# Residual of six blocks: one accumulating DMA for each block, in place of GpSimd's adds

## The chip, the core and the metric

The kernel runs on one core of one Trainium2 chip. The core has five engines that work side by side and wait for one another by semaphores: TensorE (PE in the profile) multiplies matrices into PSUM, VectorE (DVE) and ScalarE (ACT) empty PSUM and do elementwise work, GpSimd (POOL) does elementwise work and issues DMAs, and SyncE (SP) issues DMAs. DMAs move data between HBM (where inputs and outputs lie) and SBUF, and within SBUF. The metric is the device time of one execution in microseconds, the median over runs. A profile is of one execution; its span runs from the first to the last instruction.

## The reference

Attention with 16 beacon keys in front of 576 causal keys, for 8 batches and 8 heads of width 64, then a mixer on the attention's result x (8 x 576 rows of 512):

```
scores = scale * q @ k_all.T                 # k_all: beacons, then tokens; causal mask on tokens
a      = exp(scores - max) / (sum + 1e-9)
x      = a @ v_all                            # heads side by side: (batch, 576, 512)
h      = x.T @ U @ V                          # rank 32, along the 576 tokens
u      = x + h.T
out    = u + relu(u @ w_ch1) @ w_ch2          # 512 -> 2048 -> 512, float32
```

The last line matters here: `out` is the sum of the residual u and the second layer's product. The kernel takes float32 and computes with float16 operands and float32 sums.

## The kernel before, in words

**Two streams of work.** Attention runs batch by batch and head pair by head pair. The mixer runs on the 4608 rows of all batches, in 9 blocks of 512 rows (t = 0 to 8); a block can begin when u of its rows is there. The units of the mixer's blocks (a few matmuls and what goes with them) stand in a list `queue`; `fill(n)` (L1269) takes n units from it, and the attention code calls `fill` between its own steps. So TensorE gets attention and mixer work in turn, in an order fixed when the program is built. Every engine runs its own instructions in that order.

**Two more lists go with the units.** `storing` (L1108) holds stores with a countdown: after every unit `fill` lowers the countdown of all entries, and calls those at the front that have fallen below zero. `coming` holds loads of later batches (k, q, v and beacons, all issued by GpSimd, which converts them from float32 to float16) and some sums of weights; `fill` calls one of them after every unit.

**Where u comes from.** For each batch from the third on, SyncE transposes x into the ring `uT` (L456, five DMA transposes), TensorE multiplies the low-rank part into four PSUM banks (`most`, L490) and one for the last rows (`end`, L503), and VectorE adds those onto `uT` (L477). The blocks' first layer reads `uT` as its moving operand (L675, L701).

**A block (`fast_units`, L622).** The first layer gives 2048 x 512 values `gT`, with ReLU. The second layer uses seven half-size products in place of eight (sums of operands on VectorE ahead, sums of products behind). Blocks 1 to 6 do this by `c_unit` and `after`; in blocks 7 and 8, called `quads`, another order (`chain_units`) ends the run. A block's result comes in four quarters of 256 rows x 256 columns: "11", "22", "21" and "12", in this order; a quarter is one tile `ob` (128 x 2 x 256 float32; pool `outp`, four buffers). VectorE, or ScalarE in some blocks for "11" (L926), writes the product into `ob`.

**The residual.** `out` wants u in row order. So SyncE transposes the block's part of `uT` into a float16 tile `ut` (128 x 4 x 512; pool `utp`, two buffers; L640), four DMA transposes that go out with the units of the block's first layer. `residual` (L860) then has GpSimd add the right quarter of `ut` to `ob` in four pieces of 128 columns (`in_pieces`, L571; the instruction's line is L577), and `store` (L851) puts the store of the quarter into `storing` with a countdown of 2; SyncE issues it (L854). Blocks 7 and 8 call `residual` for "11" alone; their other quarters get u by VectorE (`begun`). Block 0 has its own code (L1010) without `residual`.

**GpSimd's order.** Its queue holds, in the order in which the program was built: the loads of `coming`, the adds of `residual`, the sums of weights (L615). An add that waits for `ob` holds the loads behind it.

Of the kernel before, what the change touches and what calls it, by code (L numbers as in the profile page):

```python
# [14 lines left out]
ALU = mybir.AluOpType  # L15
# [3 lines left out]
P = 128  # L19
# [11 lines left out]
def kernel(  # L31
# [13 lines left out]
    nc = tc.nc  # L45
# [525 lines left out]
    def in_pieces(o, x, y, op, n=4):  # L571

        h = o.shape[1]
        w = o.shape[2] * h // n
        for i in range(h):
            for c in range(0, o.shape[2], w):
                nc.gpsimd.tensor_tensor(  # L577
                    out=o[:, i, ds(c, w)], in0=x[:, i, ds(c, w)], in1=y[:, i, ds(c, w)], op=op
                )
# [42 lines left out]
    def fast_units(t0, dst, last=False, parts=0, ahead=None):  # L622


        cell, banks, obs = {}, {}, {}
        few = PARTS.get(t0 // 512 + 1, 0) == 1
        quads = t0 // 512 >= NBLK - 2
# [209 lines left out]
        def u_of(h, c):  # L837
            return cell["u"][:, ds(2 * h, 2), ds(HC * c, HC)]
# [12 lines left out]
        def store(name, h, c, i=None, c0=0, w=HC):  # L851
            if i is None:
                both = dst(2 * h, 2 * P)[:, ds(HC * c, HC)].rearrange("(k p) c -> p k c", p=P)
                u = lambda t=obs[name]: nc.sync.dma_start(out=both, in_=t)  # L854
                storing.append([2, u]) if not last else u()
            else:
                eng = nc.scalar if name == "21" or i and not c0 else nc.sync
                eng.dma_start(out=dst(2 * h + i, P)[:, ds(HC * c + c0, w)], in_=obs[name][:, i, ds(c0, w)])

        def residual(name, h, c):  # L860
            in_pieces(obs[name], obs[name], u_of(h, c), ALU.add)
            store(name, h, c)

        def after(k):
            if k == 0:
                nc.scalar.activation(out=kept("s1"), in_=banks["A"], func=AF.Copy)
                freed("A")
            elif k == 1:
                add(out_tile("11"), banks["F"], cell["s1"])
                freed("F")  # L870
                residual("11", 0, 0)
            elif k == 2:
                add(kept("u2"), banks["B"], cell["s1"])
                freed("B")
            elif k == 3:
                add(kept("u3"), banks["C"], cell["u2"])
                freed("C")
            elif k == 4:
                add(out_tile("22"), banks["D"], cell["u3"])
                residual("22", 1, 1)  # L880
            elif k == 5:
                add(out_tile("21"), banks["E"], cell["u3"])
                freed("E")
                residual("21", 1, 0)
            else:
                add(out_tile("12"), banks["D"], cell["u2"])
                freed("D")
                residual("12", 0, 1)
# [219 lines left out]
    coming, storing = [], []  # L1108
# [186 lines left out]
    def feed(b):  # L1295

        while state["t"] < NBLK and 512 * (state["t"] + 1) <= S * (b + 1):
            t = state["t"]
            dst = lambda i, m, t=t: rows[ds(512 * t + P * i, m), :]
            if t < FAST:  # L1300
                units, state["part"] = mlp_units(512 * t, 512, dst, t % 2, t > 0)
                if t == FAST - 1:
                    for i, u in zip(DIFFS, halves_of_w2()):
                        units[i] = lambda a=units[i], u=u: (a(), u())
            else:
                units = fast_units(512 * t, dst, t == NBLK - 1, PARTS.get(t, 0), sums_ahead(t + 1))
            queue.extend(units)
            state["t"] += 1
# [40 lines left out]
    with tc.manual_schedule(engines={ENG.PE, ENG.Activation, ENG.DVE, ENG.SP, ENG.Pool}):  # L1349
# [191 lines left out]
        for p in range(NP1, NP):  # L1541
            b, c = divmod(p, NH2)
# [127 lines left out]
```

## Time and profile before

| | |
|---|---|
| Median of 3 runs | 332.73 us (332.49 to 332.76) |
| The profiled execution | 332.49 us, span 330.7 us |
| Granted TensorE clock, mean | 0.996 |
| Instructions in the span | 9280 |
| HBM read, written | 37.45 MB, 9.44 MB |
| Share of the chain that ended last | PE 91%, ACT 4%, DVE 1%, DMA 1% |

How to read the rows that follow. A row by group names line, engine, operation, output <- inputs (names of tiles, buffer numbers left out), shapes, count, then busy time in us, mean ns of one instruction, and the engine's idle time just before them with what ended it. A row of the timeline or of the chain begins with its start and its length in us. A row of waits reads: who, at which line, waited for what: total us, times, longest. A DMA row gives the issuing queue, the count, the size and the median us from issue to landing. In a table by stretches each engine's busy time is followed by its number of instructions. Queue q0 carries GpSimd's DMAs, q1 those of SyncE.

### The profile page before, as it was taken

How to read it: one execution, taken by the hardware profiler on the slowest of the kernel's cores; microseconds unless marked ns; L12 is line 12 of the kernel's file. 1: busy time of each engine (PE TensorE's matmuls, PEld its weight loads, DVE VectorE, ACT ScalarE, POOL GpSimd, SP SyncE). 2: the span in 40 equal slices, each digit the busy share in tenths (PEclk: the TensorE clock that was granted, in tenths of full speed). 3: DMA queues.
4: the chain of work that ended last, by engine and by line, in shares of the span. 5: the costliest groups of instructions: out<-in, count | busy, mean ns of one | idle time of the engine just before them, and what ended most of it. 6: DMA issues, size and time to landing. Idle time of an engine off the chain costs nothing.

```text
span 330.7 us, 9280 instructions
## 1 busy us (share of the span) xinstructions
PE 322.6 (98%) x3660; PEld 228.1 (69%) x3660; DVE 264.7 (80%) x608; ACT 196.4 (59%) x430; POOL 166.7 (50%) x263
## 2 busy tenths in 40 slices
PE   7899999999999999999999999999999999999994
PEld 3564555555578656876588888765787888788783
DVE  6776988679998668786878777877788898798993
ACT  5957962789972677348844695379636613703700
POOL 8987724766238960689058923950283036030030
PEclk9999999999999999999999999999999999999998
DMA  7999999999999996999999999995014313405003
GB/s 164 142 179 143 185 201 194 200 187 155 80 129 166 215 130 106 111 162 138 148 149 162 146 135 160 92 211 81 10 65 120 70 44 101 63 11 166 18 10 125
DMA packets 150561, 41.99 MB, mean 127 GB/s; under 512 B 131312, under 2 KB 149936, under 8 KB 150512
## 3 DMA queue, kind: packets, MB, share of 16 engines
q0 software_dynamic: 87568, 18.18, 73.1%
q1 hardware_dynamic: 62144, 22.41, 37.4%
q10 hardware_dynamic: 800, 0.75, 0.7%
q8 instruction: 30, 0.49, 0.7%
q14 instruction: 19, 0.16, 0.2%
HBM read 37.45 MB, written 9.44 MB: 142 GB/s over the span
## 4 chain that ended last, share of the span: by engine, by line
PE 91%; ACT 4%; DVE 1%; DMA 1%; issue 0%; ACTq 0%
PE gps L675 21%; PE mpsA L909 9%; PE po L428 8%; PE qpsA L701 6%; PE mpsD L829 6%; PE sps L410 6%; PE cps L1053 4%; PE gps L1027 4%; PE mpsE L829 3%; PE mpsC L829 3%; PE mpsB L829 3%; PE qpsD L701 3%; ACT expt L377 2%; PE mpsF L829 2%; PE mpsD L909 2%; ACT w L377 2%
## 5 line engine op out<-in xcount | busy, mean ns | idle before, releaser
L577 POOL TENSOR_TENSOR ob<-ob,ut 128x128 f32<-128x128 f32 x104 | 50.0, 511 | 121.9 <-DVE ob L849 59.4
L419 ACT ACTIVATE expt<-sps 128x496 f16<-128x496 f32 (+2 forms) x192 | 82.0, 539 | 41.8 <-PE sps L410 41.8
L675 PE MATMUL gps<-uT,w 128*128 128x512 f16 (+1 forms) x368 | 78.1, 351 | 0.0
L829 PEld LDWEIGHTS <-gT 128*128 128x128 f16 x576 | 54.2, 98 | 8.8 <-issue 2.6
L675 PEld LDWEIGHTS <-w 128*128 128x128 f16 x368 | 33.2, 98 | 25.6 <-issue 1.3
L653 DVE TENSOR_TENSOR gT<-gT 128x1024 f16<-128x1024 f16 (+3 forms) x87 | 47.0, 561 | 0.9
L239 POOL DMA_DIRECT2D vs<-in_v_dram x50 | 39.9, 811 | 14.1 <-DMA w<-in_moe_w_ch_dram 11.6
L683 ACT ACTIVATE gT<-gps 128x512 f16<-128x512 f32 x63 | 37.4, 617 | 16.1 <-PE gps L675 11.9
L428 PEld LDWEIGHTS <-expt 128*128 128x128 f16 x900 | 33.9, 98 | 8.4 <-issue 1.5
L428 PE MATMUL po<-vs,expt 128*128 128x65 f16 x900 | 36.4, 194 | 0.6 <-DVE expt L349 0.4
L909 PEld LDWEIGHTS <-gT 128*128 128x128 f16 x336 | 31.2, 98 | 4.0
L437 DVE TENSOR_TENSOR xb<-po,rec 128x320 f16<-128x320 f32 x64 | 31.4, 491 | 2.2
L349 DVE TENSOR_TENSOR expt<-expt,bigmask 128x768 f16<-128x768 f16 x56 | 31.3, 598 | 0.4 <-ACT expt L419 0.2
L720 ACT ACTIVATE kept<-qpsA 128x512 f32<-128x512 f32 x18 | 10.9, 603 | 24.0 <-PE qpsA L701 13.2
L410 PE MATMUL sps<-qT,kT 64*128 64x80 f16 (+4 forms) x288 | 22.6, 281 | 0.0
L436 DVE RECIPROCAL rec<-po 128x5 f32<-128x5 f32 x64 | 11.9, 186 | 12.4 <-PE po L428 12.1
L377 ACT ACTIVATE expt<-sps 128x496 f16<-128x496 f32 (+2 forms) x48 | 20.6, 572 | 0.6 <-PE sps L371 0.6
L909 PE MATMUL mpsA<-w,gT 128*128 128x256 f16 x160 | 19.1, 273 | 0.0
L410 PEld LDWEIGHTS <-kT 64*128 64x128 f16 x288 | 10.2, 94 | 12.8 <-issue 8.2
L681 DVE TENSOR_SCALAR gT<-gps 128x512 f16<-128x512 f32 x17 | 11.7, 688 | 8.5 <-PE gps L675 8.2
L1126 POOL DMA_DIRECT2D st<-in_k_dram x20 | 16.9, 860 | 1.4 <-DVE xb L437 1.4
L1126 POOL DMA_DIRECT2D st<-in_q_dram x20 | 17.0, 877 | 0.2 <-DVE expt L349 0.2
(159 smaller groups left out, 540.4 us busy)
## 6 DMA issues: line engine op xcount, KB each, us to landing
out_dram<-ob SPq DMA_DIRECT2D x33, 256.0 KB, 3.4
vs<-in_v_dram POOLq DMA_DIRECT2D x18, 128.0 KB, 7.2
w<-in_moe_w_ch_dram POOLq DMA_DIRECT2D x4, 512.0 KB, 6.6
w<-in_moe_w_ch_dram POOLq DMA_DIRECT2D x2, 1024.0 KB, 13.1
st<-in_k_dram POOLq DMA_DIRECT2D x12, 128.0 KB, 6.3
st<-in_q_dram POOLq DMA_DIRECT2D x12, 128.0 KB, 8.3
st<-in_k_dram POOLq DMA_DIRECT2D x4, 288.0 KB, 11.5
st<-in_q_dram POOLq DMA_DIRECT2D x4, 288.0 KB, 12.5
```

What stands on the lines that cost most here:

```text
L239: nc.gpsimd.dma_start(out=dst[a : a + nq[j], j, :, :], in_=src[hs, ds(q0[j], nq[j]), :].rearrange("h p d -> p h d"))
L377: nc.scalar.activation(out=ex[i][:, ds(AT[g], gw[g])], in_=ps[g, i][:, 0 : gw[g]], func=AF.Exp, scale=scale)
L410: nc.tensor.matmul(banks[i][:, ds(at0 + o, w)], kT(hp, c, ch), qT[hp, c, ds(qa, w)], start=True, stop=True, skip_group_check=len(unit) > 1,)
L419: nc.scalar.activation(out=at[p][3][i][:, ds(AT[g], gw[g])], in_=bank[:, ds(at0, gw[g])], func=AF.Exp, scale=scale)
L428: nc.tensor.matmul(po[:, j, :], ex[0 : nk[c], ds(blk[(c, j)], P)], vs[0 : nk[c], ds(c * H * E + h * E, E)], start=(c == 0), stop=(c == j),)
L577: nc.gpsimd.tensor_tensor(out=o[:, i, ds(c, w)], in0=x[:, i, ds(c, w)], in1=y[:, i, ds(c, w)], op=op)
L653: nc.vector.tensor_tensor(out=o[:, ds(d0, n)], in0=x[:, ds(d0, n)], in1=y[:, ds(d0, n)], op=op)
L675: nc.tensor.matmul(g[:, ds(o, w)], w1[:, cc, ts(dc, P)], uT[:, cc, ds(at, w)], start=(cc == 0 and o == 0), stop=(cc == NCC - 1), skip_grou ...
L683: nc.scalar.activation(out=cell["g"][:, dc, :], in_=g, func=AF.Relu)
L829: nc.tensor.matmul(ps, a()[:, d, ds(P * i, P)], bm[:, d, ds(c0, w)], start=fresh and d == 0 and i == 0, stop=d == HF - 1, skip_group_check ...
L909: nc.tensor.matmul(ps, a()[:, d, ds(P * i, P)], bm[:, d, ds(c0, w)], start=fresh and d == 0, stop=d == HF - 1, skip_group_check=True,)
L1126: coming.append(lambda d=dst, s=src, a=m[j] - nq[j], n=m[j], j=j: nc.gpsimd.dma_start(out=d[a:n, j, :, :], in_=s[:, ds(q0[j], nq[j]), :].r ...
```

## The change

In blocks 1 to 6 `residual` no longer adds: a quarter is stored as the product alone. Behind the store of "12", the block's last quarter, one more entry goes into `storing`, with a countdown of 8: a DMA issued by GpSimd, whose source is the block's whole `ut` tile (128 x 4 x 512, float16) and whose destination is the block's 512 rows of `out` (float32), with `accum_op=ALU.add`. It converts u to float32 and adds it to what the four stores have put there; it waits for these stores. Blocks 7 and 8 (`quads`) keep their adds.

```diff
         def residual(name, h, c):
-            in_pieces(obs[name], obs[name], u_of(h, c), ALU.add)
+            if quads:
+                in_pieces(obs[name], obs[name], u_of(h, c), ALU.add)
             store(name, h, c)
+            if name == "12":
+                storing.append([8, lambda: nc.gpsimd.dma_start(
+                    out=dst(0, 4 * P).rearrange("(k p) c -> p k c", p=P), in_=cell["u"], accum_op=ALU.add
+                )])
```

## The prediction

> **What bounds the kernel now.** I read first the page's busy times and slices, then each engine's busy time by stretches of the span, then the chain of work that ended last, in order of time.
>
> ```profile
> PE 322.6 (98%) x3660; PEld 228.1 (69%) x3660; DVE 264.7 (80%) x608; ACT 196.4 (59%) x430; POOL 166.7 (50%) x263
> DMA  7999999999999996999999999995014313405003
> ```
> ```profile
> 165.00:200.00 35.00, 35.00 (x439) 28.98 (x437) 28.02 (x61) 22.27 (x50) 21.18 (x33) 1.00 1.74 149
> ...
> sum 231.00, PE 231.00 PEld 176.22 DVE 188.51 ACT 125.96 POOL 104.18; mean PE 33.00 PEld 25.17 DVE 26.93 ACT 17.99 POOL 14.88
> ```
> ```profile
> 205.25 0.57 PE po L428 x15
> 205.81 1.75 PE mpsC L829 x16
> 207.56 0.14 PE uend L503 x4
> ...
> 213.74 0.86 PE gps L675 x4
> ```
>
> The second fence is the table by stretches (length, then busy time of PE, weight loads, DVE, ACT, POOL, then granted clock, DMA share, GB/s). Its seven stretches run from 95 to 326 us, and PE is busy for 231.00 of 231.00 us, at a granted clock of 1.00. A busy PE could still be a slow PE, so the chain has to confirm it. In the third fence each piece begins where the one before it ends (205.25 + 0.57 = 205.82, 205.81 + 1.75 = 207.56), and sixteen 256-column matmuls take 1.75 us, 109 ns each; the other pieces of sixteen take 1.75 to 1.85. So from 95 us to 326 us, which is the whole stretch that the change touches, TensorE alone sets the time. DVE, ACT and POOL all have room. The DMA engines are the second fullest resource: 9 tenths in nearly every slice up to about 224 us, a share of 1.74 (overlapping packets count twice) from 165 to 200.
>
> **What goes.**
>
> ```profile
> L577 POOL TENSOR_TENSOR ob<-ob,ut 128x128 f32<-128x128 f32 x104 | 50.0, 511 | 121.9 <-DVE ob L849 59.4 <-ACT ob L926 56.1 <-ACT expt L419 5.5
> SPq L854 <- POOL ob L577: 29.9, 18, 3.1
> ```
>
> Each of blocks 1 to 6 has four results of four adds: 96 of the 104. That is 96 x 0.511 = 49 us of GpSimd's time, and nearly all of the 29.9 us in which SyncE's queue stood at a store until the adds were done. Neither is on PE's path: not one piece of the chain between 95 and 326 us is of another engine. What this work delays, and what its absence can hurry, is already hidden. Gain on the path: 0.0 us. Blocks 7 and 8 keep their 8 adds, and the last store is untouched.
>
> **What moves.** GpSimd runs its instructions in order, so a waiting add also held the loads behind it.
>
> ```profile
> 120.86 0.55 POOL L221 DMA_DIRECT2D vs<-in_beacon_v_dram  x1 [0.56 <-PE po L428]
> 134.98 1.58 POOL L577 TENSOR_TENSOR ob<-ob,ut 128x128 f32<-128x128 f32 x4 [13.57 <-DVE ob L849]
> 136.51 4.23 POOL L239 DMA_DIRECT2D vs<-in_v_dram  x5
> ...
> 148.00 1.65 POOL L577 TENSOR_TENSOR ob<-ob,ut 128x128 f32<-128x128 f32 x4
> 149.60 3.40 POOL L1126 DMA_DIRECT2D st<-in_k_dram  x4
> 152.96 4.22 POOL L1126 DMA_DIRECT2D st<-in_q_dram  x5
> ```
>
> Here the five loads of v at 136.51 stood behind an add that waited 13.57 us for DVE. Without the adds they can follow the beacon load at once, at about 121.4, and the k and q loads follow them, 10 to 20 us earlier than now. By itself that is more slack, not less. But these loads then fly while SyncE transposes the next rows of u; that is rival 1.
>
> **What is added.** Six times: one DMA issued by GpSimd, which reads u (512 KB in f16), reads 1 MB of stored rows, adds, and writes 1 MB. Its issue costs GpSimd what its other loads cost (4.22 us for five: 0.84 us); 6 x 0.84 = 5 us on an engine that just lost 49. Its flight is not in the trace. The nearest rows:
>
> ```profile
> out_dram<-ob SPq DMA_DIRECT2D x11, 256.0 KB, 2.2
> out_dram<-ob ACTq DMA_DIRECT2D x3, 128.0 KB, 1.8
> w<-in_moe_w_ch_dram POOLq DMA_DIRECT2D x2, 1024.0 KB, 13.1
> ```
>
> The first is of 236 to 300 us, the second of the tail, the third of the whole run. Doubling a store from 128 to 256 KB adds 0.4 us, so 1 MB would take 2.2 + 6 x 0.4 = 4.6 us if the read of the old rows were free, and 2.2 + 14 x 0.4 = 7.8 us if it cost as much as the write. The widest converting load, among other traffic, took 13.1 us. That load moves 3 MB in all, the new DMA 2.5. I take 8, the stores' rate with the read counted, since the stores are the rows that write to the same place; 4.6 and 13.1 are the ends, and a far end follows as rival 2. The Trainium skill (DMA: Bandwidth & Descriptors, "Anatomy of one DMA — SWDGE (gpsimd) path") gives 2.0 us plus bytes over 436 GB/s: as an estimate 4.4 us for 1 MB, 6.8 us if the read counts too; no run here shows an accumulating DMA, and the sum would be the same by it.
>
> The new DMA has to wait until the four stores of its block have landed.
>
> ```profile
> out_dram<-ob SPq DMA_DIRECT2D x33, 256.0 KB, 3.4
> ```
> ```profile
> 115.25 0.59 SPq L854 DMA_DIRECT2D out_dram<-ob  x1
> ...
> 149.67 0.44 SPq L854 DMA_DIRECT2D out_dram<-ob  x1
> ...
> 167.89 6.72 SPq L1148 DMA_TRANSPOSE qT<-st  x5
> ```
>
> The store of "12" goes at 115.25 in block 1 and at 149.67 in block 2, both held for GpSimd's adds until then; a store flies 3.4 us. Some 1.5 us earlier without the adds, the last store lands near 118 and 151. The new entry of `storing` is called eight units after the store's own unit, and each unit takes one load off `coming`. So eight of the nine k and q loads that follow the add at 148.00 stand ahead of the new DMA of block 2 on GpSimd, and one behind it. GpSimd, running ahead, reaches it at about 135 and stands there for some 16 us. Behind it wait only that last q load and the next beacon load (which goes at 157.56 in the profile). SyncE turns the five q tiles from 167.89 on, so a load issued at 152 is in time. Block 3 has the same order one block later; in block 1 and blocks 4 to 6 only work for a later batch is behind. The u tile (two buffers) is held until the DMA has landed, and the next transposes into that buffer come a whole block, over 30 us, later. Cost on the path: 0.0 us.
>
> **The sum.** 0 gained, 0 paid. The profiled execution took 332.49 us (span 330.7, 1.8 around it), 0.24 below the median of 332.73, within the spread of the three runs. I predict the median, **332.7 us**. A difference of 0.2% (0.7 us) is about what a measurement of this kernel can tell from none.
>
> **Rival 1: late transposes of u (slower).**
>
> ```profile
> q0 software_dynamic: 7248, 0.91, 128.0%
> uT<-xb SPq DMA_TRANSPOSE x5, 7.6
> L456 SPq DMA_TRANSPOSE uT<-xb x5: 1185/1265/1841, 156.5 to 162.2; - x5
> DMA to landing us min/median/max: 5.9/7.6/8.6
> ```
> ```profile
> uT<-xb SPq DMA_TRANSPOSE x5, 2.5
> ```
> ```profile
> L456 SPq DMA_TRANSPOSE uT<-xb x5: 1259/1265/2067, 193.3 to 199.4; - x5
> DMA to landing us min/median/max: 3.8/6.2/8.2
> ```
> ```profile
> 171.26 2.40 DVE L477 TENSOR_TENSOR uT<-ups,uT 128x496 f16<-128x496 f32 x4
> 205.64 2.40 DVE L477 TENSOR_TENSOR uT<-ups,uT 128x496 f16<-128x496 f32 x4
> ```
>
> With GpSimd's queue busy (155 to 167 us) a transpose of x into uT lands after 7.6 us; without it (222 to 236 us) after 2.5. DVE adds onto uT at L477, in order, and holds four PSUM banks until it has. The last transpose lands at 162.2 + 5.9 = 168.1 for the add at 171.26, a margin of 3.1 us; at 199.4 + 3.8 = 203.2 for 205.64, a margin of 2.4. These two boundaries are the tightest. If v's loads, moved forward, lengthen the 3.8 to 7.6, the add at 205.64 comes 207.0 - 205.64 = 1.4 us late. If half of the new DMA's 8 us is added to every transpose instead, 4 - 3.1 = 0.9 and 4 - 2.4 = 1.6 are paid: 2.5 us, **335.2 us**; with all 8 us, 4.9 + 5.6 = 10.5, 343. It decides from a delay of 2.4 us. Against it: block 5's first matmul on the new u comes at 213.74, 5.7 us after these adds end (208.04), so a late add stops PE only through the banks; and the new DMA of block 2 (near 151) starts 5 us before the transposes at 156.5. The Trainium skill (DMA: Bandwidth & Descriptors, "Issuing engines are not separate DMA queues") says that DMAs of all issuers run on the same 16 engines and interleave: by that rule the moved loads and the new DMA do lengthen the transposes. The trace agrees (7.6 against 2.5 us).
>
> **Rival 2: the accumulate goes row by row (much slower).** 512 rows over 16 engines are 32 rows each. If each row's read and write had to finish before the next, at the 1.8 us that the smallest store group above shows, one DMA took 58 us, longer than a block. v's loads stand behind it in the same queue:
>
> ```profile
> 153.07 0.46 PE po L428 x15
> vs<-in_v_dram POOLq DMA_DIRECT2D x18, 128.0 KB, 7.2
> ```
>
> PE reads the next v at 153.07. The new DMA of block 1 starts near 118 and the loads need 4.2 + 7.2 us after it, so it decides from a flight of about 153 - 11.4 - 118 = 24 us; at 58 PE stands 34 us in this block alone: **366 us** or more. Against it: converting loads of as many bytes take 13.1.
>
> **Rival 3: faster.**
>
> ```profile
> L653 DVE TENSOR_TENSOR gT<-gT 128x1024 f16<-128x1024 f16 x41 | 29.0, 719 | 0.1
> ```
>
> These take 0.68 us where GpSimd does not add beside them, 0.719 in the mean: 41 x 0.04 = 1.6 us of DVE's time come back, and at the very best, if DVE's time were PE's, **331.1 us**. The Trainium skill (SBUF — State Buffer, "Who interferes with whom") has a DVE instruction with two SBUF inputs and a GpSimd instruction that reads SBUF shut each other out. Against the gain: PE waits for nothing in that stretch.
>
> That the adds do not go is no case: the row of L577 will tell (x8).
>
> **Chances.** Forecast 0.70; rival 1 0.20, rival 2 0.05, rival 3 0.05. So faster 0.05, same 0.70, slower 0.25. The range, 332.0 to 336.5 us, takes in the forecast's own spread (332.5 to 332.8 in the runs shown) and rival 1 with half of the new DMA's flight or somewhat more; rival 2, rival 1's far end and rival 3 are left out, some 0.15.
>
> **What would show it.** Right: L577 at x8, v's loads at about 121 to 126 us, no wait of SyncE for GpSimd at L854, a flight of 5 to 13 us for the six new DMAs, PE still busy for all of 95 to 326 us. Wrong: a wait of PE at a bank after L477, L477 itself later than 171.26 and 205.64, or "po" waiting for a load of v, which means that the flight is over 24 us.

## The result, and the profile after

The changed kernel takes 345.53 us (median of four runs, 342.76 to 347.57) where the kernel before takes 332.63 on the same chip: a ratio of 1.0383, with an interval of 1.0292 to 1.0473. On a second chip it took 347.58 against 332.45 (1.0464; 1.0447 to 1.0482). It is slower by some 13 to 15 us, and outside the predicted range. Every ratio in this text leaves out runs that took over 1.5% longer than the fastest of the same kernel: one each of x1, x2 and x10 below, the highest of their ranges. The profiled execution of the changed kernel took 347.32 us, with a span of 345.7; before it was 330.7, so 15.0 us are to be found. Of lines that moved, L1126, L1142 and L1148 of before are L1131, L1147 and L1153 now; the new DMA is L865.

The page of the changed kernel, busy times and the slices of the DMA engines:

```profile
PE 327.6 (95%) x3660; PEld 229.9 (67%) x3660; DVE 263.2 (76%) x608; ACT 197.6 (57%) x430; POOL 132.5 (38%) x173
DMA  8999999999999999999999999968304832905103
```

The table by stretches (length, then busy time of PE, weight loads, DVE, ACT and POOL, then granted clock, DMA share, GB/s):

```profile
95.00:130.00 35.00, 33.05 (x341) 21.19 (x340) 22.71 (x48) 19.14 (x45) 18.62 (x22) 0.95 1.56 166
130.00:165.00 35.00, 32.52 (x356) 23.15 (x353) 23.34 (x54) 19.68 (x44) 9.72 (x13) 1.00 1.66 150
165.00:200.00 35.00, 30.62 (x339) 23.11 (x338) 23.11 (x51) 17.49 (x39) 13.05 (x17) 0.95 1.79 150
200.00:235.00 35.00, 33.70 (x409) 26.08 (x407) 29.83 (x57) 21.06 (x48) 14.41 (x14) 1.00 1.30 170
```

TensorE had no gap from 95 to 326 us before. Now it stands in each of the four stretches up to 235 us (1.95, 2.48, 4.38 and 1.30 us), and in two of them its mean clock is 0.95. From 270 us on it is full again. GpSimd is busy for 34 us less (166.7 to 132.5 us), and that bought nothing. What TensorE waits for, by the table of waits:

```profile
PE sps L410 <- DMA qT<-st: 8.8, 3, 4.3
...
PE sps L410 <- DVE xb L437: 1.2, 1, 1.2
```

Neither the new DMA nor the transposes of u stand first. Three times the scores (`sps`, L410) wait for a tile of `qT`: q of a later batch, which GpSimd loads into `st` and SyncE then transposes. TensorE's timeline at the first and the third of these stops:

```profile
116.37 0.39 PE L410 MATMUL sps<-qT,kT 64*128 64x496 f16 x2 [1.95 <-DMA qT<-st]
116.69 3.80 PE L675 MATMUL gps<-uT,w 128*128 128x512 f16 x9
```
```profile
194.50 0.39 PE L410 MATMUL sps<-qT,kT 64*128 64x496 f16 x2 [4.33 <-DMA qT<-st]
...
195.99 3.28 PE L675 MATMUL gps<-uT,w 128*128 128x256 f16 x16
```

And by short stretches, the same columns as above:

```profile
115.00:120.00 5.00, 3.63 (x11) 1.36 (x12) 1.03 (x2) 2.18 (x5) 0.00 (x0) 0.69 1.30 202
150.00:155.00 5.00, 2.83 (x44) 1.89 (x39) 3.98 (x10) 2.19 (x4) 0.00 (x0) 1.00 1.76 158
193.00:200.00 7.00, 5.50 (x35) 4.15 (x36) 0.00 (x0) 2.83 (x6) 0.00 (x0) 0.76 2.09 183
```

A stop costs more than its own length. After the first, nine 512-column matmuls take 3.80 us, 0.42 each (in the kernel before, seventeen of them took 3.84 us from 114.41 on, 0.23 each); after the third, sixteen of 256 columns take 3.28 us, 0.2 each, where the prediction's chain had 0.109. The granted clock of these stretches is 0.69 and 0.76. The second stop, 2.48 us at 152.8, was followed by no slow matmuls.

Matching each of the 3660 matmuls with the same one of before gives the whole account. At the three stops the delay grows by 2.11, 2.65 and 4.49 us (9.3); behind the first and the third it grows by another 1.70 and 1.56 while the clock is low (3.3); four times DVE is late, 0.34, 0.43, 1.49 and 0.44 us (2.7). With 0.16 us that was there long before the first stop the sum is 15.4 us, 0.4 more than the difference of the spans; the run's end gives that back.

**Why q came late.** SyncE's timeline, k and q of the second such set, before and after:

```profile
129.28 1.97 SPq L1142 DMA_TRANSPOSE kT<-st  x1
131.38 7.96 SPq L1148 DMA_TRANSPOSE qT<-st  x5
```
```profile
133.55 8.11 SPq L1147 DMA_TRANSPOSE kT<-st  x1
142.19 8.11 SPq L1153 DMA_TRANSPOSE qT<-st  x5
```

And the flights of these five transposes, before and after:

```profile
L1148 SPq DMA_TRANSPOSE qT<-st x5: 1199/1355/1804, 131.4 to 138.1; - x5
...
DMA to landing us min/median/max: 2.5/4.1/6.2
```
```profile
L1153 SPq DMA_TRANSPOSE qT<-st x5: 1183/1228/2096, 142.2 to 149.1; - x5
...
DMA to landing us min/median/max: 7.6/8.4/8.9
```

The issue of one transpose of k grew from 2 to 8 us, the q tiles behind it in SyncE's order went out 11 us later (4 of them are the delay of the first stop), and their median flight doubled. The matmuls of each stop begin 0.14 us after the fourth of the five q tiles has landed (at 116.24, 155.18 and 194.36). In the kernel before, that tile was there 2.6, 7.3 and 5.2 us ahead of the same matmuls. GpSimd's timeline shows what flew beside them:

```profile
122.40 1.34 POOL L865 DMA_DIRECT2D out_dram<-ut  x1 [13.29 <-DMA out_dram<-ob]
...
125.39 4.21 POOL L239 DMA_DIRECT2D vs<-in_v_dram  x5
...
140.58 0.82 POOL L1131 DMA_DIRECT2D st<-in_q_dram  x1 [1.29 <-DMA vs<-in_v_dram]
...
163.07 1.31 POOL L865 DMA_DIRECT2D out_dram<-ut  x1 [17.70 <-issue]
```

In the kernel before, the loads of v began at 136.51 and those of k and q at 149.60, behind the adds: the transposes of q (131.38 to 139) had none of these loads beside them until 136.51. Now v goes at 125.39 and k and q from 131.26 to 145.4, all of it beside the transposes. From 145.4 on GpSimd stands at the new DMA until the stores of block 2 have landed, and the loads behind it (the last q, the beacons, five of v, then k of the next batch) go from 163.9 on, beside the third set of transposes, which SyncE issues from 171.00 to 188.4. That is the stop of 4.33 us. The first stop comes before any new DMA is issued: its q tiles flew 7.4 to 9.0 us, against 4.3 to 6.2 before, beside loads of k and q that ran from 94.2 to 104.4 us in place of 101.1 to 113.6.

**Why DVE came late.** DVE's timeline before, DVE's after, and GpSimd's after:

```profile
194.00 1.02 DVE L349 TENSOR_TENSOR expt<-expt,bigmask 128x768 f16<-128x768 f16 x2
```
```profile
207.14 2.94 DVE L349 TENSOR_TENSOR expt<-expt,bigmask 128x768 f16<-128x768 f16 x2
```
```profile
206.74 1.50 POOL L615 TENSOR_TENSOR st<-st,w 128x512 f16<-128x512 f16 x1
208.20 1.46 POOL L615 TENSOR_TENSOR st<-w 128x512 f16<-128x512 f16 x1
```

GpSimd's sums of weights run at the same time as before (205 to 211 us), but DVE's work is 13 us late by now, and its masks (L349) fall on them: the pair takes 2.94 us instead of 1.02.

The new DMA itself and the loads, by the page's table of DMA issues (queue, count, size, median us to landing):

```profile
out_dram<-ut POOLq DMA_DIRECT2D x6, 1024.0 KB, 9.0
...
st<-in_k_dram POOLq DMA_DIRECT2D x12, 128.0 KB, 11.6
st<-in_q_dram POOLq DMA_DIRECT2D x12, 128.0 KB, 13.2
```

### The profile page after: what moved, and what is told of

It reads as the page before. It is cut to its first block, busy times and chain, and to the rows that moved or that the text cites. A ratio compares the mean times of both kernels' runs of the same rounds, so it can differ in the third digit from the quotient of the medians.

```text
span 345.7 us, 9186 instructions
## 1 busy us (share of the span) xinstructions
PE 327.6 (95%) x3660; PEld 229.9 (67%) x3660; DVE 263.2 (76%) x608; ACT 197.6 (57%) x430; POOL 132.5 (38%) x173
## 3 DMA queue, kind: packets, MB, share of 16 engines
HBM read 37.45 MB, written 15.73 MB: 154 GB/s over the span
## 4 chain that ended last, share of the span: by engine, by line
PE 69%; DMA 11%; issue 6%; DVE 6%; ACT 4%; POOL 1%; SPq 1%; ACTq 0%; POOLq 0%
PE gps L675 15%; PE mpsA L914 7%; PE po L428 6%; PE qpsA L701 5%; DMA qT<-st 5%; DMA vs<-in_v_dram 5%; PE cps L1058 4%; PE sps L410 4%; PE mpsD L829 4%; PE gps L1032 3%; PE qpsD L701 3%; PE mpsC L829 3%; PE mpsB L829 3%; ACT expt L377 2%; PE mpsF L829 2%
## 5 line engine op out<-in xcount | busy, mean ns | idle before, releaser
L675 PE MATMUL gps<-uT,w 128*128 128x512 f16 (+1 forms) x368 | 80.9, 362 | 0.0
L675 PEld LDWEIGHTS <-w 128*128 128x128 f16 x368 | 34.6, 101 | 27.2 <-issue 3.2
L865 POOL DMA_DIRECT2D out_dram<-ut x6 | 7.9, 1316 | 114.5 <-DMA out_dram<-ob 96.8
L653 DVE TENSOR_TENSOR gT<-gT 128x1024 f16<-128x1024 f16 (+3 forms) x87 | 47.3, 565 | 0.9
L349 DVE TENSOR_TENSOR expt<-expt,bigmask 128x768 f16<-128x768 f16 x56 | 33.5, 638 | 0.3 <-ACT expt L419 0.2
L410 PE MATMUL sps<-qT,kT 64*128 64x80 f16 (+4 forms) x288 | 24.0, 281 | 10.1 <-DMA qT<-st 8.8
L410 PEld LDWEIGHTS <-kT 64*128 64x128 f16 x288 | 10.6, 94 | 23.8 <-issue 17.5
L720 ACT ACTIVATE kept<-qpsA 128x512 f32<-128x512 f32 x18 | 10.8, 601 | 24.1 <-PE qpsA L701 13.5
L1131 POOL DMA_DIRECT2D st<-in_k_dram x20 | 16.8, 850 | 16.6 <-DMA vs<-in_v_dram 9.6
L681 DVE TENSOR_SCALAR gT<-gps 128x512 f16<-128x512 f32 x17 | 11.7, 688 | 13.7 <-PE gps L675 13.5
L723 DVE TENSOR_TENSOR gT<-qpsD,kept 128x512 f16<-128x512 f32 x12 | 8.3, 689 | 18.1 <-ACT kept L720 16.7
L1131 POOL DMA_DIRECT2D st<-in_q_dram x20 | 17.9, 907 | 4.4 <-DMA vs<-in_v_dram 2.9
```

What stands on the lines that cost most here:

```text
L349: nc.vector.tensor_tensor(out=e, in0=e, in1=bigmask[:, :, :].rearrange("p (a b) x -> p a b x", b=2), op=ALU.min)
L410: nc.tensor.matmul(banks[i][:, ds(at0 + o, w)], kT(hp, c, ch), qT[hp, c, ds(qa, w)], start=True, stop=True, skip_group_check=len(unit) > 1,)
L653: nc.vector.tensor_tensor(out=o[:, ds(d0, n)], in0=x[:, ds(d0, n)], in1=y[:, ds(d0, n)], op=op)
L675: nc.tensor.matmul(g[:, ds(o, w)], w1[:, cc, ts(dc, P)], uT[:, cc, ds(at, w)], start=(cc == 0 and o == 0), stop=(cc == NCC - 1), skip_grou ...
L1131: coming.append(lambda d=dst, s=src, a=m[j] - nq[j], n=m[j], j=j: nc.gpsimd.dma_start(out=d[a:n, j, :, :], in_=s[:, ds(q0[j], nq[j]), :].r ...
```

## The experiments

The trace offered three theories, which need not exclude one another. **Loads** (theory M in the forecasts): the cost is in the loads that left their place when the adds went; it has nothing to do with the accumulate. **DMA** (theory D): the six new transfers delay others (rival 1 of the prediction, or the q tiles). **Sums** (theory S): GpSimd's sums of weights meet DVE's masks. Each experiment is told as an edit of `residual` or of its new DMA. Ratios are those of the comparison with the kernel before on the same chip, whose median was 332.45 to 332.75 us; they aren't quotients of the medians.

| run | what | median us (low to high) | ratio (95%) |
|---|---|---|---|
| x1 | adds gone, no DMA | 340.61 (340.27–347.51) | 1.0202 (1.0109–1.0295) |
| x2 | adds kept, DMA added | 334.71 (333.39–342.69) | 1.0067 (1.0026–1.0107) |
| x3 | change, all four waits kept | 334.18 (332.33–335.64) | 1.0030 (0.9993–1.0066) |
| x4 | change in blocks 4 to 6 only | 335.31 (333.99–336.68) | 1.0054 (1.0022–1.0086) |
| x5 | x4, four sums not computed | 334.92 (333.69–335.72) | 1.0076 (1.0054–1.0098) |
| x6 | no DMA, k and q held, v free | 333.85 (333.54–337.12) | 1.0052 (1.0016–1.0087) |
| x7 | no DMA, one wait a block | 332.43 (331.94–332.76) | 0.9988 (0.9975–1.0002) |
| x8 | x3 without the add | 331.98 (one run) | |
| x9 | change, one wait a block | 333.86 (332.44–335.48) | 1.0034 (1.0019–1.0049) |
| x10 | DMA to rows stored long ago | 352.68 (349.69–355.77) | 1.0641 (1.0568–1.0714) |
| x11 | the change again, beside x10 | 347.58 (345.42–348.36) | 1.0464 (1.0447–1.0482) |

**x1: the loads alone.** The adds go and nothing takes their place.

```diff
             store(name, h, c)
-            if name == "12":
-                storing.append([8, lambda: nc.gpsimd.dma_start(...)])
```

> No adds and no accumulating DMA in blocks 1 to 6: these rows come out without the residual. What is left of the change is that GpSimd's loads are no longer held behind adds that wait for results. Theory M (the moved loads share the DMA engines with SyncE's transposes of q and k, and PE stops at sps L410): the first stop of the changed kernel, 2.0 us at 116.4 us and before the first accumulating DMA, comes back together with about 1.5 us of slow clock behind it, and others follow; 336 to 345 us. Theory D (the new DMA's own 9 us of traffic, six times, is the cause): 332.5 to 333.5 us, no wait of PE for qT. Both needed: 334 to 338 us.

With no new DMA at all the kernel is still 2.0% slower. TensorE's timeline, and the flights of the second set of q:

```profile
116.56 0.39 PE L410 MATMUL sps<-qT,kT 64*128 64x496 f16 x2 [2.18 <-DMA qT<-st]
```
```profile
L1149 SPq DMA_TRANSPOSE qT<-st x5: 1184/1214/3430, 140.4 to 147.9; - x5
...
DMA to landing us min/median/max: 7.1/8.7/9.6
```

The first stop is the changed kernel's, and so is the low clock behind it (1.7 us more); the transposes of the second set fly 8.7 us. The stops at the other two places are shorter: 1.11 us at 154.12 and 0.39 at 188.89. The row of 154.12 names ACT, but the fourth q tile, issued at 144.39 with a flight of 9.6 us, landed 0.14 us before it, as at the stops whose rows name the tile. Further stops, of 0.4 to 1.2 us, come behind DVE from 197 to 212. So the moved loads alone cost about half of what the change does, and the accumulate has no part in that.

**x2: the DMA alone.** All adds stay, and the six DMAs run besides (u is added twice in blocks 1 to 6).

```diff
-            if quads:
-                in_pieces(obs[name], obs[name], u_of(h, c), ALU.add)
+            in_pieces(obs[name], obs[name], u_of(h, c), ALU.add)
```

> The kernel before with all its adds, and the six accumulating DMAs beside them: u is added twice in blocks 1 to 6. The loads stay held by the adds. Theory M: 332.5 to 333.5 us, as the transposes of q land before PE needs them. Theory D: 342 to 347 us, with waits of PE for qT at two or three batches. Both needed: 334 to 338 us, a stop at sps where the DMA's flight falls upon the transposes of q (block 2 and block 3), none at 116 us.

DVE's timeline:

```profile
173.16 2.42 DVE L477 TENSOR_TENSOR uT<-ups,uT 128x496 f16<-128x496 f32 x4 [1.65 <-DMA uT<-xb]
...
208.14 2.42 DVE L477 TENSOR_TENSOR uT<-ups,uT 128x496 f16<-128x496 f32 x4 [1.52 <-DMA uT<-xb]
```

These are the two adds that rival 1 named, late for the reason it named. TensorE loses 0.8 and 0.7 us there. No stop for a q tile is left, since the loads are where they were. The time lies in the range of "both needed", but that forecast had the stops at the q tiles.

**x3: the change with its old pace.** At each quarter GpSimd copies one column of `ob` to a scratch tile: it waits where the adds made it wait, and computes nothing.

```diff
             if quads:
                 in_pieces(obs[name], obs[name], u_of(h, c), ALU.add)
+            else:
+                nc.gpsimd.tensor_copy(out=warm, in_=obs[name][:, 0, 0:1])
```

> The changed kernel, and in place of each of the 96 adds' groups one copy of a single column of the result into a scratch column by GpSimd, which waits for the result as the add did. So the loads are held as before, without the adds' work; the accumulating DMAs stay. Theory M: 332.5 to 333.5 us, a kernel as fast as before. Theory D: 342 to 347 us. Both needed: as with the DMAs beside the adds, 334 to 338 us, within 1 us of that run, since the adds' own work does not matter.

All that is left of the 13 us is 0.3%, with an interval that reaches no change; the median is within 1 us of x2's, as "both needed" has it. In the profiled execution (332.43 us) TensorE has no stop in the stretch at all; the transposes of x into `uT` land at 171.07, 0.6 us ahead of DVE's add at 171.70. In other runs that margin may be gone (up to 335.64); no trace shows one of these.

**x4 and x5: blocks 4 to 6 only, then without one set of sums.** By the prediction's account only work for a later batch moves in these blocks.

```diff
-            if quads:
+            if quads or t0 < 4 * 512:
...
-            if name == "12":
+            if name == "12" and t0 >= 4 * 512:
```

> Blocks 1 to 3 as before (adds, no DMA), blocks 4 to 6 as changed. The loads of later batches end at about 222 us, so the DMA engines have room behind that. Theory M and theory D both: 332.5 to 333.5 us, no wait of PE; if it is slower by more than 0.5 us, the cause is not the fullness of the DMA engines but something in the new DMA itself (a wait of SyncE for u's tile, or of PE).

It came out slower than forecast, and showed the third theory. DVE, GpSimd and TensorE in its timeline:

```profile
196.46 2.93 DVE L349 TENSOR_TENSOR expt<-expt,bigmask 128x768 f16<-128x768 f16 x2
```
```profile
197.51 1.46 POOL L615 TENSOR_TENSOR st<-w 128x512 f16<-128x512 f16 x1
```
```profile
204.73 0.39 PE L410 MATMUL sps<-qT,kT 64*128 64x336 f16 x5 [1.18 <-DVE xb L437]
```

Here the sums themselves moved: they stood behind an add (205.31 in the kernel before) and now run from 194.81. DVE's pair of masks takes 2.93 us, DVE is late with x, and TensorE loses 2.0 us. (Another 2 us of this one trace were lost near 15 us, where the two programs are the same.) x5 takes that set of sums away: the tile is filled with zeros.

```diff
-nc.gpsimd.tensor_tensor(out=o, in0=x, in1=y, op=op)
+nc.gpsimd.memset(o, 0.0) if q == 1 else nc.gpsimd.tensor_tensor(out=o, in0=x, in1=y, op=op)
```

> Blocks 4 to 6 changed as in the run of the late blocks, and the four sums of weights of block 7's second set (L615, two inputs from SBUF) are plain writes of zero by GpSimd, so block 7 and 8 compute with wrong sums. Theory S (moved forward from about 205 to 195 us, these sums shut out DVE's instructions with two inputs from SBUF: L349 in pairs 2.93 us instead of 1.02): the pair at L349 near 196 us takes 1.0 to 1.1 us again, the stop of PE at sps behind it (2.0 us) is gone, 332.5 to 333.5 us. Theory D' (the three late accumulating DMAs themselves): as slow as the run of the late blocks, 334.5 to 336 us, with the stop near 204 us.

```profile
194.17 1.02 DVE L349 TENSOR_TENSOR expt<-expt,bigmask 128x768 f16<-128x768 f16 x2
```
```profile
192.79 1.95 POOL L616 MEMSET st<- 128x512 f16 x4
```

The masks take 1.02 us again, beside or right behind a GpSimd that only writes, and the stop near 204 is gone. The time isn't: the next set of sums, begun at 223.88, makes DVE late again (an instruction of L730 in its kernel takes 1.44 us at 224.42, and 0.63 at 189.69; TensorE loses 0.9 us at 226.55), and the runs of x4 and x5 overlap. So the mechanism is shown in the trace, its price in the median isn't. The Trainium skill (SBUF — State Buffer, "Who interferes with whom") has a DVE instruction with two SBUF inputs contend with a GpSimd instruction that reads SBUF, and not with one that only writes; the trace agrees on both, 2.93 us against 1.02.

**x6 and x7: which loads must be held.** Without the new DMA, x6 puts the waits of x3 only where they hold loads of k and q (v is free to move); x7 puts one wait in each block, at the first quarter.

```diff
+            elif name in {1: ("11", "22", "21"), 2: ("21",), 3: ("21",), 4: ("11",)}.get(t0 // 512, ()):   # x6
+            elif name == "11":   # x7
+                nc.gpsimd.tensor_copy(out=warm, in_=obs[name][:, 0, 0:1])
```

> No adds and no accumulating DMA in blocks 1 to 6 (rows without the residual there); a one-column copy by GpSimd holds the queue at three results of block 1, at '21' of blocks 2 and 3 and at '11' of block 4. So the loads of k and q and the sums of weights are held as in the kernel before, and the ten loads of v of two batches run 10 to 15 us ahead. If the loads of k and q are what collides: 332.5 to 333.5 us. If the loads of v do as well (they fly while x is transposed into uT): 334 to 336 us, with a wait of DVE for uT at L477. As slow as with all loads free (340): neither is the point.

> As the run with the loads alone, but a one-column copy by GpSimd holds the queue at the first result, '11', of each of blocks 1 to 6. The loads of v go when they went before; those of k and q follow them at once, 6 us ahead of before rather than 17. The DMA engines' transposes of q and k are then mostly issued already. Theory M: most of the 8 us comes back, 332.5 to 334 us; the transposes of q land within 6 us. If the holding at the other three results matters too: 336 us or more.

x6 falls between its two forecasts. With v's loads 15 us ahead (121.78), its second set of q tiles flew 2.3 to 4.3 us, and no stop for a q tile is left; so the loads that collide are those of k and q. It loses some 1.5 us near 218, where DVE's masks take 1.98 us beside sums of weights that now run from 212.84: the third theory again. x7 is back at the time of before, 0.9988 (0.9975 to 1.0002): 24 quarters without adds, six waits of 0.2 us of work each, and nothing lost or gained. The flights of its third set of q:

```profile
L1151 SPq DMA_TRANSPOSE qT<-st x5: 1204/1227/2054, 166.4 to 172.6; - x5
...
DMA to landing us min/median/max: 2.4/4.1/6.1
```

This is the cleanest pair of the study: x1 and x7 differ in six tiny instructions, whose part here is to wait, and in about 2% of the time, each measured against the kernel before on its own chip.

**x8: what the add costs the DMA.** x3 with a plain write: u replaces the stored rows.

```diff
-out=dst(0, 4 * P).rearrange("(k p) c -> p k c", p=P), in_=cell["u"], accum_op=ALU.add
+out=dst(0, 4 * P).rearrange("(k p) c -> p k c", p=P), in_=cell["u"]
```

> The run with the one-column copies, but the six DMAs write u over the stored rows in place of adding it (no read of the old rows). Measures the flight. If reading the old rows costs as much as writing: the quiet ones (blocks 5 and 6) land after 5 us in place of 8.4 to 9.1. If the rows are limited by the packets of the widening copy: 7.5 us or more. The time is that of the run with the copies, 332 to 335 us.

The tables of DMA issues of x3 and of x8:

```profile
out_dram<-ut POOLq DMA_DIRECT2D x6, 1024.0 KB, 9.5
```
```profile
out_dram<-ut POOLq DMA_DIRECT2D x6, 1024.0 KB, 5.7
```

Adding onto the old rows, in place of writing over them, makes the flight longer by about two thirds. The two quiet ones, of blocks 5 and 6, took 5.3 and 6.0 us against 9.1 and 8.7 in x3: nearer to the first of the two explanations. That it is the read isn't shown: the pages count 37.45 MB read from HBM in both runs, as in the kernel before. One run of x8 took 331.98 us, which doesn't prove a difference from x3.

**x9: the change with one wait a block.** The accumulate with x7's single wait, as the candidate for a better version.

```diff
+            elif name == "11":
+                nc.gpsimd.tensor_copy(out=warm, in_=obs[name][:, 0, 0:1])
```

> The changed kernel with its accumulating DMAs and one one-column copy by GpSimd at '11' of each of blocks 1 to 6, which holds the loads as the first add did. Theory M with a smaller share for the new DMA: the loads of k and q are issued by 148 us, so the new DMA of block 2 starts near 151 instead of 156 and has landed by about 160, before the last transposes of x; 332.4 to 333.5 us, no stop of PE, faster than or equal to the run with four copies (334.2). If the new DMA's own traffic costs PE time wherever it flies: 333.5 to 335 us, with a late L477 at 171 or 206 us as in the run with the DMAs beside the adds.

```profile
207.41 2.42 DVE L477 TENSOR_TENSOR uT<-ups,uT 128x496 f16<-128x496 f32 x4 [1.39 <-DMA uT<-xb]
```
```profile
219.60 0.39 PE L410 MATMUL sps<-qT,kT 64*128 64x496 f16 x2 [1.19 <-ACT expt L419]
```

It is slower by 0.34% (0.19 to 0.49), the second of the two forecasts, and x7 without the DMA is not: about 1.2 us are the price of the six transfers themselves. The DMAs of blocks 2 and 3 went at 156.39 and 192.09, later than assumed because the block's stores landed later, and fell on the transposes of u; the add at L477 is late by 1.39 us. The larger stop, at 219.60, is a q tile once more, though its row names ACT: SyncE, slowed at the transposes of u, issued the fourth set of q from 207.09 (203.40 before), beside v's loads (208.72 on), and the fourth tile flew 8.5 us and landed 0.13 us before the stop ended. No version of this study beats the kernel before.

**x10 and x11: is it the standing?** x1 and x9 together give about 2.4%; the change costs 3.8 to 4.6. One explanation was left: GpSimd stands 11 to 18 us at the new DMA, holds the loads behind it, and releases them together onto the transposes of q. x10 sends the accumulate to the rows of the block before, stored long ago, so that there is nothing to stand for; x11 is the change itself.

```diff
-out=dst(0, 4 * P).rearrange(
+out=dst(-4, 4 * P).rearrange(
```

> The change with one edit: the accumulating DMA of a block goes to the rows of the block before (so its 512 rows get this block's u, and the output is another). Same bytes, same place in GpSimd's order, but these rows were stored some 35 us earlier, so GpSimd need not stand at it (13.29, 17.70 and 11.58 us in the changed kernel) and the loads behind it are not held. Theory 'standing' (the 4 us that neither the moved loads alone nor the DMA alone gave come from loads held behind that wait, which then fall together on the transposes of q at 179 to 187): no idle time over 3 us before L865, no stop of TensorE of 4 us for a qT tile near 194; about the 340.6 of the loads alone plus the 1.2 of the DMA: 340.5 to 343. Rival 'flights' (a flight of 9 us in a queue already full costs this wherever it starts): 344 to 348, as the changed kernel, with the stops at other places. A result below 340 would say that the held loads cost more than that.

> The changed kernel unaltered, on the same chip, as the measure for the run beside it: 343 to 348 by both theories.

Both forecasts failed: x10 is slower than the change by some 5 us. GpSimd's and TensorE's timelines, and the page's DMA row:

```profile
141.79 1.31 POOL L865 DMA_DIRECT2D out_dram<-ut  x1 [0.95 <-DMA uT<-xb]
```
```profile
161.82 0.59 PE L410 MATMUL sps<-qT,kT 64*128 64x496 f16 x2 [8.72 <-DMA qT<-st]
```
```profile
out_dram<-ut POOLq DMA_DIRECT2D x6, 1024.0 KB, 13.5
```

The standing is indeed gone (0.95 us at block 2), and so is the 4 us stop near 194. But the new DMA now goes out at 141.79, ahead of the transposes of q (143.7 to 152), and they fly 8.0 to 13.3 us beside it: a single stop of 8.72 us, with the low clock behind it (the delay grows by another 1.8). So it isn't the standing as such. In the traces of x1, x10 and the change, every stop for a q tile follows transposes that flew 7 us or more beside GpSimd's transfers. x11 stops at the same three places as the first trace of the change (the delay grows by 2.0, 2.3 and 4.8 us).

## Why the prediction was wrong, by its own steps

**"What bounds the kernel now"** held. TensorE without a gap is what x7 gives back, at the same time. It also meant that an input which is late by more than its own margin costs all the rest, and with a low clock behind the stop more than that, since no slack in TensorE can swallow it.

**"What goes"** held as far as it went: L577 is at x8, the 29.9 us in which stores waited for GpSimd's adds are down to 3.1, and x7 shows the gain on the path, 0.0.

**"What moves" is the step that failed**: "By itself that is more slack, not less", with a price of nothing. The forecast put the loads 10 to 20 us earlier and v's at 121.4; they moved so (v at 125.39 instead of 136.51). But it asked only whether the moved loads are in time themselves, not who flies beside them. For the q tiles it checked the source ("a load issued at 152 is in time") and not the transposes: their issue times (131.38 and 167.89) and flights (2.5 to 6.2 us) stood in the trace of before, as did TensorE's next use of q. Worked out as rival 1 does it, the first set gives a margin of 2.6 us: the fourth tile, issued at 105.55, landed at 111.48 for a matmul at 114.10. That is as tight as the two boundaries which the prediction called the tightest. In the change this tile landed at 116.24. The step measured, by x1 against before, 2.0% (1.1 to 3.0) in place of nothing.

**"Cost on the path: 0.0 us" for the new DMA** failed by a smaller sum: 0.34% in x9, 0.67% in x2, 0.3% in x3 with an interval that reaches zero. The flight was well sized (8 taken, 4.6 to 13.1 as bounds; 9.0 measured as the median, 8.4 to 9.9 for the six). Its issue was put too low (0.84 us; 1.31 measured), on an engine that had room. The wait came out right by luck (16 us forecast for block 2; 17.70), since both its ends are 10 to 12 us later than forecast. Its place was wrong: the DMA of block 2 went at 163.07, not near 151, because SyncE's queue, behind its own slow transposes, issued the last store at 154.92 and the stores flew 7 to 8 us. "Behind it wait only that last q load and the next beacon load" left out v's loads and the next batch's k, which also stood there once the DMA was 12 us later.

**Rival 1** had the right mechanism for the DMA: L477 late for `uT`, at the two boundaries it named, 1.65 and 1.52 us late in x2 with 1.5 us lost, against its 2.5. In the change itself that is 0.34 of 15.4 us; that its far end, 343, lies near the result is chance. It looked at one of SyncE's two kinds of transposes, the one with a margin of 2.4 to 3.1 us; the other, with a first margin of 2.6, was hit harder. **Rival 2** fell: the accumulate is a transfer of 9 us. **Rival 3** came out on the other side: DVE's L653 gained nothing (565 ns in the mean of all its shapes, 561 before), and GpSimd's remaining sums met DVE's masks (2.94 us for 1.02), which cost instead of gave.

What stays open is the split of the rest. The moved loads (about 2.0%) and the DMA with loads held (about 0.3 to 0.7%) leave some 1 to 2.5% of the change that appears only when both are there. That remainder is loosely known: the interval of x1 alone reaches 3.0%, and its highest time, 347.51 us, is that of the change without any new DMA; no trace shows that run. The traces of the change and of x10 place the remainder at the transposes of q; no run separates the DMA's bytes from the loads that it releases.

## What to carry to other kernels

An engine that computes in order and also issues DMAs sets the pace of those DMAs: taking its waiting work away moves the transfers behind it, and here earlier was not free, since the DMA engines were nearly full. Before such a change is priced, list each transfer of other queues that flies in the stretch which the moved loads enter, with its flight now and the margin to its reader; the shortest margin decides, whoever owns it. Where the work must go, keep its wait: one instruction of 0.2 us a block was worth 2% here.

## What the runs showed that was not expected

- SyncE's transposes slow down a lot beside GpSimd's loads. Their flight went from 2.5 to 6.2 us to 7.6 to 8.9, and SyncE's issue of one transpose of k from 2 to 8 us; with an accumulating DMA just ahead, 8.0 to 13.3.
- GpSimd stands at some of its own loads. In the change it stands ten times, up to 2.4 us, at a load of k or q, and by the profile until a load of v has landed (the wait of 1.29 us at 140.58 is one). Why is not shown.
- An accumulating DMA of 512 KB of float16 onto 1 MB of float32 rows flew 8.4 to 9.9 us in the change. It flew 13.5 in the median, and up to 20.5, when it went out among the loads (x10). As a plain write (x8) it flew 5.7 in the median.
- A stop of 1.95 us was enough for a low clock (0.69 from 115 to 120 us), and one of 2.48 us was not (1.00). In x11 stops of 1.79 and 2.09 us were followed by the full clock too (1.00 from 116.3 to 121 and from 153.2 to 158), in x1 one of 2.18 us by 0.63 (116.5 to 121). So the length of the stop alone does not decide it in these traces. The Trainium skill (TensorE: Matmul & The Clock Gate, "Part 1: The HAM clock gate") has TensorE drop to half speed after an idle window of about 3.4 us and come back after as long a busy one. The length of the slow stretch agrees (3.80 us at 0.42 us a matmul); a stop of 1.95 us is shorter than that window, and there the measurement decides.
